# Blocks 3 to 5: half of the first product by 49 small products instead of 7 large ones

## The chip, the core and the metric

The kernel runs on one NeuronCore of a Trainium2 chip. TensorE (PE) multiplies matrices; VectorE (DVE), ScalarE (ACT) and GpSimd (POOL) do elementwise work; SyncE (SP) issues DMAs, and so do the queues of ACT and POOL. Matrix products land in PSUM, which has eight banks of 128 x 512 fp32; everything else lies in SBUF, or in DRAM (HBM). The metric is the device time of one execution in microseconds, as the median of the runs; lower is better.

## What is computed

```
state = gamma * state + k_t^T v_t          (4 batches, 8 heads, 768 steps, head size 64)
y_t   = (q_t state) / 8
x = y as (3072 tokens, 512)
h = x @ w_in                               (512 x 2048)
out = (h * sigmoid(1.702 h)) @ w_out       (2048 x 512)
```

All in fp32. The recurrence is computed in chunks of 128 steps (small attention-like products, 64x64); the two large products take most of the time.

## The kernel before, in words

Tokens are worked in six blocks `m` = 0 to 5 of 512 tokens (as four quarters). Chunk steps of the recurrence that make x for a later block are run between units of work of the current block (`between`, L968 to L980: `step` and `turn`).

**First product ("up").** w_in is laid out as eight column blocks `p`; two of them make a pair `d` (0 to 3). Of x and of w_in, four quadrants are held, plus sums of them, so that a 2x2 block product takes seven products instead of eight (P1 to P7, a Strassen-Winograd scheme; `sums_x` L529 makes the sums of x, `sums_w1` L521 those of w_in). In blocks 2 to 5, `up(d)` (L555 to L597) runs the seven products of a pair, each of four matmuls with 256 columns (L562), adds the results in PSUM and in SBUF (ACT copies P1, P6 and P7 out, L569, L576, L583; DVE adds, L572, L580, L586, L588), applies the gate x*sigmoid(1.702x) on ACT (`hidden`, L393), and lastly makes, on DVE, the sums of the gated values that the second product needs (L594, L595 inside 128-column parts, L596, L597 between the four quadrants `G[.., s, :]`). In this text those are "presums" and "outer sums".

The last two pairs' weights (`W1B`) share their room with `ring` and `own`, the buffers of the second product; so from block 3 on they are fetched again from DRAM (`W1D`, L984, L988) on POOL's queue, 1792 KB each.

**Second product ("down").** In blocks 2 to 5, `down49` (L643) goes one level deeper: each of the seven products is again split by seven, so 49 products of 128x128x128 parts. A unit is half of one of the seven: four products or three of them, each of four matmuls with 128 columns (`products`, L662 to L667). `derive(i)` (L651) makes three sums of G on DVE for product i; the three sums of w_out are streamed from DRAM (`stream`, L632, 768 KB). Results are copied by ACT (`then`, L698) or added by DVE and POOL and stored (`put`, L683). `sums_g_outer` (L621) are further DVE sums between units. After units 1, 4, 7 and 10 a chunk step stands in the order of PE.

**Order.** PE runs in the order in which the program is written. For the other engines a planner orders the instructions at compile time, by program order and by when it reckons each to be ready; `keep_in_program_order` (`pin`, L118, while `ordered[0]` holds) keeps an instruction in its written place among the others so marked on its engine. Each engine runs its list strictly in order.

PSUM: two banks of tag x and two of tag y (`ps`), two double banks `pa` and `py` for the chunk steps (`ps_a`).

## Time and profile before

| what | us |
|---|---|
| runs (median of 3) | 658.35 (658.05, 658.35, 664.67) |
| span of the profiled execution | 660.5 |
| PE busy | 642.2 (97%) |
| DVE / ACT / POOL busy | 453.9 / 159.0 / 198.8 |
| block 3, first product (362.90 to 411.20) | 48.3 |
| block 3, second product with chunk steps (411.20 to 464.70) | 53.5 |
| block 5, second product, no chunk steps (613.20 to 660.50) | 47.3 |

The page gives no time of the profiled execution but its span, which is 2.15 us over the median of the runs; differences between stages are read from the span's clock. A fp32 matmul shows as two records, so the counts of matmuls in a row are twice those in the code. The duration of one instruction is longer than the distance between two of them when they overlap in the pipeline.

### The profile page before, as it was taken

The page shows a single profiled execution, that of the slowest core. Times are in us where ns is not written, and L with a number is a line of the kernel's source. Part 1 is how long each engine was busy: PE and PEld are TensorE (multiplying, and loading weights), DVE is VectorE, ACT ScalarE, POOL GpSimd, SP SyncE. Part 2 cuts the span into 40 slices and gives each one's busy share as a digit, 9 for nine tenths or more (in the row PEclk, how much of TensorE's full clock was granted, in tenths as well). Part 3 has the DMA queues.
Part 4 walks back from the last instruction along what each step waited for, and adds up shares of the span by engine and source line. Part 5 has one row for each costly group of instructions (what it writes and reads, how often), then busy time and mean ns, then how long its engine had stood idle before and what let it go on. Part 6 is the DMA issues. An engine that isn't in the chain of part 4 may idle for free.

```text
span 660.5 us, 15291 instructions
## 1 busy us (share of the span) xinstructions
PE 642.2 (97%) x6390; PEld 580.2 (88%) x6390; DVE 453.9 (69%) x645; ACT 159.0 (24%) x306; POOL 198.8 (30%) x225
## 2 busy tenths in 40 slices
PE   6789999999999999999999999999999999999997
PEld 3778888888788888889999888999888999988997
DVE  3699989999936973556984445995354995254965
ACT  4674233551000000333100233010233110233110
POOL 6400311310379217000536400445600255500000
PEclk9989999999999999999999999999999999999999
DMA  9995549763233556262485832386742252602142
GB/s 176 193 274 173 152 104 241 172 163 60 49 82 135 137 149 153 58 248 96 118 199 134 279 57 97 86 223 135 225 118 97 66 154 104 235 21 96 55 154 96
DMA packets 148149, 91.86 MB, mean 139 GB/s; under 512 B 131600, under 2 KB 134416, under 8 KB 147056
## 3 DMA queue, kind: packets, MB, share of 16 engines
q1 hardware_dynamic: 135856, 45.19, 29.8%
q0 software_dynamic: 9888, 44.46, 20.6%
q10 hardware_dynamic: 2336, 1.25, 0.6%
q8 instruction: 50, 0.82, 0.5%
q14 instruction: 19, 0.16, 0.1%
HBM read 72.89 MB, written 15.47 MB: 134 GB/s over the span
## 4 chain that ended last, share of the span: by engine, by line
PE 89%; DVE 4%; DMA 4%; SPq 1%; issue 1%; ACT 0%; DVEq 0%
PE pq L666 27%; PE px L562 17%; PE pd L799 13%; PE py L562 13%; PE ph L491 7%; PE ph L414 5%; PE pa L289 2%; PE py L312 2%; PE pa L297 2%; PE py L306 2%; DMA W<-in_moe_w_in_dram 1%; DMA W<-in_moe_w_out_dram 1%; DMA q_in<-in_q_dram 1%; PE pt L250 1%; SPq L140 1%
## 5 line engine op out<-in xcount | busy, mean ns | idle before, releaser
L635 POOL DMA_DIRECT2D ring<-W2D x28 | 15.4, 551 | 227.7 <-PE px L562 118.3
L666 PE MATMUL pq<-W,G 128*128 128x128 f32 x672 | 80.2, 276 | 0.0
L666 PEld LDWEIGHTS pq<-W,G 128*128 128x128 f32 x672 | 77.6, 192 | 1.3 <-issue 0.7
L666 PE MATMUL pq<-ring,own 128*128 128x128 f32 x448 | 60.1, 276 | 1.3 <-issue 1.3
L562 PE MATMUL px<-X,W1A 128*128 128x256 f32 x256 | 59.8, 379 | 0.0
L562 PE MATMUL px<-X,W1B 128*128 128x256 f32 x256 | 59.8, 379 | 0.0
L666 PEld LDWEIGHTS pq<-ring,own 128*128 128x128 f32 x448 | 54.5, 192 | 0.4
L562 PEld LDWEIGHTS px<-X,W1B 128*128 128x128 f32 x256 | 48.5, 190 | 6.7
L562 PEld LDWEIGHTS px<-X,W1A 128*128 128x128 f32 x256 | 48.4, 190 | 6.5
L393 ACT ACTIVATE G<-G 128x512 f32<-128x512 f32 x60 | 37.4, 628 | 54.7 <-DVE G L572 33.4
L799 PE MATMUL pd<-W,G 128*128 128x256 f32 x224 | 49.6, 381 | 0.0
L799 PEld LDWEIGHTS pd<-W,G 128*128 128x128 f32 x224 | 42.2, 190 | 5.9
L562 PE MATMUL py<-X,W1A 128*128 128x256 f32 x192 | 45.4, 379 | 0.0
L562 PE MATMUL py<-X,W1B 128*128 128x256 f32 x192 | 45.4, 379 | 0.0
L562 PEld LDWEIGHTS py<-X,W1A 128*128 128x128 f32 x192 | 36.5, 190 | 5.0
L562 PEld LDWEIGHTS py<-X,W1B 128*128 128x128 f32 x192 | 36.5, 190 | 5.0
L580 DVE TENSOR_TENSOR t<-py,u 128x512 f32<-128x512 f32 x16 | 11.1, 692 | 32.3 <-PE py L562 32.3
L569 ACT ACTIVATE p<-px 128x512 f32<-128x512 f32 x16 | 9.6, 597 | 96.0 <-PE px L562 96.0
L414 PE MATMUL ph<-X,W1A 128*128 128x256 f32 x128 | 30.6, 397 | 0.9 <-DVE X L347 0.9
L594 DVE TENSOR_TENSOR G<-G 128x512 f32<-128x512 f32 (+2 forms) x24 | 12.3, 513 | 25.7 <-ACT G L393 25.7
L666 PE MATMUL pq<-ring,G 128*128 128x128 f32 x224 | 29.6, 275 | 0.0
L666 PE MATMUL pq<-W,own 128*128 128x128 f32 x224 | 29.6, 275 | 0.0
(237 smaller groups left out, 1226.0 us busy)
## 6 DMA issues: line engine op xcount, KB each, us to landing
ring<-W2D POOLq DMA_DIRECT2D x28, 768.0 KB, 4.8
W1B<-W1D POOLq DMA_DIRECT2D x6, 1792.0 KB, 9.8
W<-in_moe_w_in_dram SPq DMA_DIRECT2D x12, 512.0 KB, 5.9
W<-in_moe_w_out_dram SPq DMA_DIRECT2D x10, 512.0 KB, 5.8
out_dram<-o POOLq DMA_DIRECT2D x20, 256.0 KB, 3.0
q_sq<-in_q_dram SPq DMA_DIRECT2D x144, 32.0 KB, 2.1
k_sq<-in_k_dram SPq DMA_DIRECT2D x144, 32.0 KB, 2.1
v_in<-in_v_dram SPq DMA_DIRECT2D x72, 64.0 KB, 3.1
```

The lines of the kernel that those rows point to most:

```text
L289: pe.matmul(pa[HALF[w], u, 0, s, :], kt[HALF[u], w, s, :], qt[HALF[u], w, s, :], start=True, stop=True)
L297: pe.matmul(pa[HALF[u], w, 1, s, :], kd[HALF[w], HP * u + s, :], vn[HALF[w], HP * u + s, :], start=True, stop=True)
L306: pe.matmul(py[HALF[o], u, 1, 2 * w + s2, :], old[HALF[u], w, 2 * s2 + o, :], qt[HALF[u], w, 2 * s2 + o, :], start=True, stop=True)
L312: pe.matmul(py[HALF[o], w, 0, 2 * u + s2 if f < NEW else 2 * s2 + u, :], vn[HALF[w], HP * u + s, :], a[HALF[w], u, s, :], start=True, stop ...
L393: pin(act.activation(g, h[:, i], AF.Gelu_apprx_sigmoid))
L414: pe.matmul(h[:, ab], w, X[:, 2 * th + c // 2, c % 2, :], start=(ab == 0 and c == 0), stop=(c == 3), skip_group_check=True)
L491: pe.matmul(acc[:, u, :], w, x, start=(start and u == 0 and c == 0), stop=(stop and c == 1), skip_group_check=True)
L562: pe.matmul(acc[:, u, :], t[:, q1 + u, sa, c, :], X[:, sb, c, :], start=(start and u == 0 and c == 0), stop=(stop and c == 1), skip_group_ ...
L594: dve.tensor_sub(q[0][1], q[0][0], q[0][1])
L635: pool.dma_start(c, W2D[i])
L666: pe.matmul(p0[:, j, :], a[:, d], w[:, d], start=(new and j == 0 and d == 0), stop=(d == NP // 2 - 1), skip_group_check=True)
L799: pe.matmul(p0[:, n, :], g1(m, p, sa)[:, n * P:(n + 1) * P], W2[:, sb, p, :], start=(new and p == 0 and n == 0), stop=(last and p == NP - ...
```

## The change

In blocks 3 to 5, pairs 0 and 1 keep their seven plain products; pairs 2 and 3 go by 49 products of 128x128x128 parts each. `up_mixed` replaces the four calls of `up`; its order on all engines is written by hand (`ordered[0] = True`). Block 2 still runs `up` for all four pairs and makes the new sums of weights for pairs 2 and 3 (`inner_w1`), which go to DRAM (`T1D`, `Q1D`).

What is added, in the order of a block:

- weights: 14 fetches of three 128x128 parts per product and pair (`fetch_t`, 192 KB each), three of the plain pairs' sums (`fetch_q(s, True)`, 512 KB each) and three more of the inner ones into the same place, all on SP; before, it was two of 1792 KB on POOL.
- sums of x for the inner level, on DVE (`inner_x`, five operations each for X0/X1, X2/X3 and X4 to X6).
- 14 plain products: P1 of pair 0, P1 of pair 1, P2 of pair 0, and so on in the order P1, P2, P6, P5, P7, P4, P3. The P1 of pair 0 is copied into the bank of P2, which accumulates on it, so one DVE addition goes.
- 14 inner products of seven matmuls with 128 columns (`quarters`), pairs 2 and 3 in turn; P1 seeds the banks of P2 the same way. Results come as seven parts, four into G and three into a buffer E; `post` adds them (five operations on two quadrants at once or on one), then `gate`, `presum`, `outer`. `post` of pair 2 is on POOL, that of pair 3 on DVE.
- the first two `derive`s of the second product are pinned into this order; its first stream goes by SP.

`down49` loses one kept sum (`t`): product 5 now accumulates in the banks of product 4. `ring`, `own` and `W1B` become one tile `LATE`, whose parts are given out by hand.

```diff
-    W1A = const.tile([P, NP // 2, 7, 2, P], F32, name="W1A")
-    W1B = [late.tile([P, 2, 7, 2, P], F32, name=f"W1B{i}", tag=f"late{i}") for i in range(2)]
+    W1A = const.tile([P, NP, 4, 2, P], F32, name="W1A")
+    LATE = late.tile([P, 2 * NP * 3, P], F32, name="LATE")
...
+    def fetch_t(k):
+        d, sw = 2 + k % 2, OF[SEQ[k // 2]][0]
+        tag = ("kT", "at", "qT", "L", "kn", "kT", "at", "M", "qT", "L", "kn", "at", "M", "L")[k]
...
+        pin(sp.dma_start(t, T1D[d][:, {5: 4, 4: 5}.get(sw, sw)]))
...
+    def up_mixed(loads, turn_next, first_stream, second_stream, derive_first, derive_second):
...
+        def quarters(p0, prod, d, half):
...
+            pairs = [(a12, b21), (s2, t2), (s3, t3), (d0, t1)] if half == 0 else [(a11, b11), (d2, t4), (d1, b22)]
+            new = prod in ("P1", "P5")
+            for j in ((0, 2, 1, 3) if half == 0 else (0, 2, 1)):
+                x, w = pairs[j]
+                pe.matmul(p0[:, j, :], w, x, start=(new and j == 0), stop=True, skip_group_check=True)
...
+        def post(eng, d, s):
...
+            pin(eng.tensor_add(top, top, m1))
+            pin(eng.tensor_add(h1u0, h1u0, h0u1))
+            pin(eng.tensor_add(one_e(2), one_e(2), h1u1))
+            pin(eng.tensor_add(h1u1, h1u1, h1u0))
+            both = at(b + 1, d, [*K, [7 * P, 2]])
+            pin(eng.tensor_add(both, both, E[:, :, 1:3] if K else E[:, k, 1:3]))
...
+        for n in range(14):
+            prod, d = SEQ[n // 2], n % 2
...
+            if prod == "P1":
+                if d:
+                    save(("p", d), "s3", x)
+                else:
+                    pin(act.activation(y, x, AF.Copy))
...
+        for k in range(14):
+            prod, d = SEQ[k // 2], 2 + k % 2
...
+            for half in range(2):
+                quarters(p0[half], prod, d, half)
+                if d == 2:
+                    evacuate(half)
+            if d == 3:
+                evacuate(0)
+                evacuate(1)
+            if prod in ("P7", "P3"):
+                s, name = (3, "v") if prod == "P7" else (2, "u")
+                for half in range(2):
+                    pin(dve.tensor_add(place(d, s, half), out(y[half], half), out(kept[name, d][half], half)))
...
+            if k == 0:
+                inner_x(1)
+            elif k in (2, 3):
+                presum(k - 2, ALL)
+                outer(k - 2)
+            elif k == 8:
+                post(pool, 2, A)
+            elif k == 9:
+                first_stream()
+                post(dve, 3, A)
+                gate(3, A)
+                gate(2, A)
+            elif k == 10:
+                turn_next()
+                presum(3, A)
+                post(pool, 2, (1,))
+            elif k == 11:
+                post(dve, 3, (1,))
+                presum(2, A)
+                derive_first()
+                gate(3, (1,))
+                gate(2, (1,))
+                loads[1]()
+            elif k == 13:
+                second_stream()
+                post(pool, 2, (2,))
+                post(dve, 3, (2,))
+                presum(3, (1,))
+                presum(2, (1,))
+                gate(3, (2,))
+                gate(2, (2,))
+                derive_second()
+                presum(3, (2,))
+                outer(3)
+                presum(2, (2,))
+                outer(2)
...
-        if m > 1:
-            if m > 2:
-                W1B[:] = [late.tile([P, 2, 7, 2, P], F32, name=f"W1B{i}", tag=f"late{i}") for i in range(2)]
-                pool.dma_start(W1B[0], W1D[0])
+        if m == 2:
             for d in range(NP // 2):
+                if d > 1:
+                    inner_w1(d)
                 up(d)
...
+        elif m > 2:
+            prev = (m + 1) * CB
+            ordered[0] = True
+            up_mixed(
...
```

`k` counts the inner products: k = 8 and 9 are P7 of pairs 2 and 3, 10 and 11 are P4, 12 and 13 are P3. `A` stands for quadrants 0 and 3. `evacuate` copies P7 to a kept buffer and P4 (quadrant 1) to G and E, both on ACT.

## The prediction

> **What bounds the kernel now.** I read the page's shares first, then the chain in order of time, then the busy times by stage.
>
> ```profile
> PE 642.2 (97%) x6390; PEld 580.2 (88%) x6390; DVE 453.9 (69%) x645; ACT 159.0 (24%) x306; POOL 198.8 (30%) x225
> ```
>
> PE is busy nearly always. The chain in order of time says how fast it goes (start, length, work; two records make a matmul):
>
> ```profile
> 409.49 1.73 PE px L562 x8
> 411.22 6.25 PE pq L666 x56
> ...
> 613.16 43.78 PE pq L666 x392
> ```
>
> A plain product of four matmuls with 256 columns takes 1.727 us (the mean of the 28 between 362.87 and 411.22), 0.432 a matmul. In the second product 196 matmuls with 128 columns take 43.78 us, 0.2234 each. From the last plain product to the first unit of the second there is no gap: the chain goes on at 411.22. The stages of block 3 (busy time of PE, PEld, DVE, ACT, POOL; clock; DMA share; GB/s):
>
> ```profile
> 362.90:411.20 48.30, 48.30 (x226) 42.51 (x225) 21.90 (x34) 16.40 (x27) 9.42 (x13) 1.00 0.49 148
> 411.20:464.70 53.50, 52.85 (x906) 52.02 (x905) 42.65 (x64) 3.87 (x7) 25.84 (x29) 1.00 0.57 140
> ```
>
> So PE is saturated in both at a granted clock of 1.00, DVE is half idle in the first product and 80% busy in the second. Why there is no gap at the seam is seen in the timeline:
>
> ```profile
> 410.91 0.43 DVE L594 TENSOR_TENSOR G<-G 128x256 f32<-128x256 f32 x1 [0.69 <-ACT G L393]
> 411.06 2.84 PE L666 MATMUL pq<-W,G 128*128 128x128 f32 x24
> 411.25 0.60 ACT L393 ACTIVATE G<-px 128x512 f32<-128x512 f32 x1 [0.37 <-PE px L562]
> 411.26 0.69 DVE L655 TENSOR_TENSOR own<-G 128x512 f32<-128x512 f32 x1
> 411.86 0.42 DVE L595 TENSOR_TENSOR G<-G 128x256 f32<-128x256 f32 x1
> 412.20 0.29 DVE L594 TENSOR_TENSOR G<-G 128x128 f32<-128x128 f32 x1
> ```
>
> Quadrant 0, which the first unit reads, was gated and presummed while the last three products still ran; one `derive` is already running. DVE then works without a pause until 436. Any DVE work that arrives late here is felt by PE.
>
> **What the change saves.** Per pair, 28 x 0.4317 = 12.09 us become 49 x 0.2234 = 10.95: 1.14 saved, 2.28 per block with two pairs, 6.85 in three blocks. That is all that PE can save, 1.04%: 651.5. The removed additions (P1 of three pairs, `t`) and POOL's two issues (0.58 each) lie beside PE and are worth nothing.
>
> **What it costs at the seam.** Let 0 be the moment when PE ends the last inner product. P7 of pair 3 (k=9) ends four products, 28 matmuls, earlier: -6.25. What follows is one chain, since the written order on ACT is copies of P7, gate of pair 3, gate of pair 2, and only then the copies of P4. A product is seen by ACT 0.19 after PE moves on (411.06 against 411.25 above). Then: second copy 0.49 (128x384, as L704), addition 0.55 (128x384, L709), `post` of pair 3 on two quadrants 2 x 0.69 + 3 x 0.42 = 2.64 (512 and 256 columns), two gates of 1024 columns at 1.17 (L207's 128x1024), first copy of P4 0.60. Sum 6.81, so it ends at +0.56. The first unit of the second product wants tag x's banks, which that copy frees: **0.56 late**. Then three copies (0.49 + 0.60 + 0.49), `post` of pair 3, quadrant 1 (2 x 0.42 + 3 x 0.29 = 1.71), and the first presum of pair 2 (0.42), which stands behind it on DVE: +4.27. PE needs it after ten matmuls, at 0.56 + 2.23 = 2.79: **1.48 more**.
>
> Unit 2 needs quadrant 1. DVE's queue before it: presum 0.42, first `derive` 3 x 0.60 (distance of such rows), four additions of P3 2.12, `post` of quadrant 2 1.71, three presums 0.87: 6.92, so +11.19. PE needs it at 2.04 + 3.57 + 2.68 (units 0, 1) + 2.0 (chunk step, 417.40 to 419.42) + 2.23 = 12.5. Bare, 1.3 us to spare; but the planner mixes the chunk step's four DVE operations (2.4) and half an outer sum (1.14, L626's distance) in between, as it mixes L655 between L594 and L595 above: **2.2 late**. Unit 4 needs the outer sums of both pairs: 0.29 + 1.80 + 0.58 + 1.41 + 0.58 + 1.41 = 6.1 bare, up to 9.3 with `put`'s additions 1.06 and two halves of outer sums 2.28; PE comes after 1.34 + 2.68 + 0.45 = 4.5. Between 1.6 and 4.8, I take **3.2**. After unit 4 DVE's list is that of before, with the derives of two products done. Sum of waits without any mutual slowing: 7.4 per block.
>
> **The shared work of POOL.** `post` of pair 2 puts two operations of 1.27 (L531, 128x512) and three of 0.74, then twice 2 x 0.74 + 3 x 0.45 = 2.8, on POOL: 10.4 us, beside DVE's densest stretch. What such neighbours do to each other:
>
> ```profile
> 368.90 0.74 POOL L694 TENSOR_TENSOR o<-o 128x256 f32<-128x256 f32 x1
> ...
> 426.37 1.64 POOL L692 TENSOR_TENSOR o<-o 128x256 f32<-128x256 f32 x1 [3.61 <-DVE o L687]
> 427.34 1.21 DVE L655 TENSOR_TENSOR own<-G 128x512 f32<-128x512 f32 x1
> 428.94 0.68 DVE L656 TENSOR_TENSOR own<-G 128x512 f32<-128x512 f32 x1
> ```
>
> Alone, the POOL operation takes 0.74 and the DVE one 0.68; beside each other 1.64 and 1.21. But over block 3's second product the loss is small: L655 to L657 lie 0.16, 0.05 and 0.05 above their 0.69 in the mean, 1.8 us for seven of each, beside some 16 us of POOL work. By that ratio 10.4 us of POOL cost DVE 1.2; if each blocked the other throughout, the gate of pair 2 would come 2.0 later (POOL's 4.8 from -6.6 and DVE's 2.64 in turn end at +0.8, and gate and copy at +2.6 instead of 0.56), and DVE would lose POOL's later 5.6 and the chunk step's 2.1 as well: nearly 10. Nearest to it is the measured ratio; with half of the 2.0, because the first two `post`s coincide from end to end, I take 2.1.
>
> SBUF — State Buffer, section "Who interferes with whom", of the Trainium skill speaks against the change: a DVE operation with two SBUF inputs and a GpSimd operation that reads SBUF exclude each other for a whole instruction. The row at 426.37 looks like that (it began to move when L628 ended at 427.34). By that rule alone the upper sum just given would hold; by the ratio the lower.
>
> **The other parts.** The plain pairs' sums (three of 512 KB) can't be fetched before the last unit of the previous block has read their place; P6 of pair 0 wants the first at 4 x 1.727 = 6.9 us. 256 KB landed in 3.0 (out), 768 KB in 4.8 (ring): about 4 plus 0.6 of issue, 2.3 to spare; rows of 512 KB at the start took 4.6 to 9.1, so the bounds are 0 and 2.8 a block. I take 0. The inner fetches have 4.7 us between the release of their place and use, three products, against 3; SP's 16 small loads (8 in 4.0 us, so 8) stand behind the first fetches and before the inner ones, which have 20 us. Block 2's added DVE work (eight operations, about 5.5) and POOL work (eight) lie in a first product where DVE is busy 25.5 of 48.4: nothing; without that cover at most the 0.6 of the last one.
>
> **Sum.** Per block 7.4 + 2.1 - 2.28 = 7.2 us; three blocks 21.7. From the span 660.5 to 682; from the median, 2.15 lower, **680**.
>
> **Rivals.** (1) *All waits are hidden*, the saving comes whole: 651.5. It is one mechanism: the planner and the pipelines shorten the chain on ACT and DVE behind P7. It decides when that chain takes 6.25 us or less to the copy of P4 and the DVE list behind it no more than PE's 2.2 us to the presum; I come to 6.81 and 3.71. For it: ACT operations follow each other at 0.48, below their 0.60. Against: the chain is of dependent steps, which don't overlap. (2) *Only the first unit waits*: 2.04 against 2.28, so 657.6, if the planner keeps the chunk steps' DVE work out; with small port losses to 664. (3) *Full mutual blocking*: with 2.0 + 2.7 + 2.7 + 2.1 for the port and unit 4 at its upper 4.8, the waits come to 18.5, net 16 a block: 707. Gaps over 3 us could also lower the granted clock, which the page shows at 9 and 8 tenths only in the first slices; the price would be the same order. (4) *Late fetches*: 2.8 a block on top, 8 us, with any of these. That the products don't become 49 would show in the count of matmul records, and I see no room for it in the code.
>
> **How the numbers follow.** The forecast (some waits at three units, 665 to 703) gets 0.66; rival 2 (652 to 664) 0.18; rival 1 0.07; rival 3 beyond 703 0.09. The range reaches from 655 to 703: it takes in the forecast and the upper part of rival 2, and leaves out the outer two. About 1% is what a measurement of this kernel tells from no change: faster than 651.8 gets 0.05 (651.5 is barely there), slower than 664.9 gets 0.75, between 0.20.
>
> **What would show it.** In the changed profile: inner products at 1.56 us each (7 x 0.2234); the first product of a block 46.1 long instead of 48.3; PE idle before the first unit of the second product, released by ACT's copy of P4, then by DVE's presum; again at units 2 and 4, released by DVE; `post` on POOL above 1.27 and 0.74. If PE shows no idle time after the seam, the chain is shorter than I sum it; if it is idle inside the plain products, the fetches are late; if POOL's `post` runs at its lone times, the share for blocking is wrong.

## The result, and the profile after

| | median us | runs | profiled span |
|---|---|---|---|
| before | 659.8 | 658.1 to 664.7 | 660.5 |
| after | 709.5 | 707.7 to 712.4 | 706.8 |

The changed kernel is slower by a ratio of 1.0755 (95% interval 1.0704 to 1.0806). The forecast was 680, its range 655 to 703. The direction was right and the time 29 us too low. Ratios here and below are to executions of the kernel before that were run beside the kernel in question (medians 659.5 to 662.5 us), without executions more than 1.5% slower than the fastest of their kernel; the medians in us are of all executions.

The page's busy times of the changed kernel, first row, with the granted clock of TensorE in 40 slices of the span:

```profile
PE 652.4 (92%) x6642; PEld 597.0 (84%) x6642; DVE 492.4 (70%) x738; ACT 174.9 (25%) x342; POOL 238.3 (34%) x269
...
PEclk9899999999999999999999999999999899998899
```

PE was busy 97% before and is 92% now, though there is less for it to do; and its clock falls to 8 tenths in slices late in the run, where it had stood at 9 or more. Where that is, the stages of block 3 say (busy time of PE, PEld, DVE, ACT, POOL, with instructions; clock; DMA share; GB/s):

```profile
368.50:414.80 46.30, 46.29 (x310) 43.05 (x308) 22.48 (x37) 16.21 (x30) 14.99 (x16) 1.00 0.57 170
414.80:418.40 3.60, 0.17 (x2) 0.00 (x0) 3.02 (x6) 2.48 (x4) 0.08 (x1) 0.96 0.11 16
418.40:434.40 16.00, 12.67 (x204) 12.11 (x204) 14.51 (x27) 4.64 (x10) 10.17 (x14) 0.90 0.58 145
434.40:445.80 11.40, 6.38 (x40) 6.19 (x40) 10.71 (x20) 0.00 (x0) 5.44 (x6) 0.83 0.56 131
445.80:450.60 4.80, 4.78 (x32) 4.67 (x32) 4.80 (x7) 0.00 (x0) 0.00 (x0) 0.69 0.45 89
450.60:484.80 34.20, 34.20 (x633) 33.76 (x633) 22.80 (x34) 2.18 (x4) 17.41 (x21) 1.00 0.67 166
```

The first product has no gap and takes 46.3 us instead of 48.3: the saving is there. The loss lies in the 36 us after it. PE's rows that begin with a wait (start, length, work; in brackets the idle time and what ended it):

```profile
418.46 3.94 PE L958 MATMUL pq<-W,G 128*128 128x128 f32 x20 [3.49 <-ACT G L840]
422.85 0.71 PE L958 MATMUL pq<-W,G 128*128 128x128 f32 x4 [0.46 <-DVE G L760]
434.47 0.71 PE L958 MATMUL pq<-W,G 128*128 128x128 f32 x4 [2.88 <-DVE G L760]
445.82 3.92 PE L958 MATMUL pq<-W,G 128*128 128x128 f32 x20 [4.96 <-DVE G L766]
...
429.09 2.50 PE L958 MATMUL pq<-W,G 128*128 128x128 f32 x20
```

The four places and their releasers are those of the prediction: ACT's copy of P4 ahead of unit 0, presums ahead of unit 0's end and of unit 2, the outer sum ahead of unit 4. They sum to 11.8 us. Note also the lengths: twenty records took 3.94 and 3.92 us behind a wait, where the twenty at 429.09, behind none, took 2.50. That is a second price of these waits.

Blocks by the first plain product on PE, in us, each from the one profiled execution of its kernel; the experiments stand below it for reference:

| kernel | block 2 begins | block 2 | block 3 | block 4 | block 5 | median, all |
|---|---|---|---|---|---|---|
| before | 261.4 | 101.3 | 101.9 | 100.1 | 95.9 | 659.8 |
| after | 268.0 | 100.5 | 116.3 | 115.1 | 106.9 | 709.5 |
| e1 stores behind | 259.5 | 100.7 | 116.5 | 115.3 | 107.0 | 701.7 |
| e2 no POOL `post` | 265.3 | 101.2 | 112.7 | 111.8 | 103.5 | 697.4 |
| e3 no `post` | 267.6 | 102.2 | 99.8 | 102.0 | 93.5 | 666.9 |
| e4 early quadrant | 259.8 | 101.0 | 116.6 | 112.2 | 103.3 | 695.3 |
| e5 all `post` on DVE | 267.4 | 100.6 | 123.0 | 116.3 | 106.2 | 710.5 |
| e6 early and late | 258.9 | 102.0 | 115.7 | 107.8 | 97.0 | 681.6 |
| e7 late others | 259.6 | 101.0 | 119.4 | 115.2 | 102.7 | 698.5 |
| e8 fill, eleven | 265.5 | 100.9 | 118.2 | 117.9 | 107.0 | 711.3 |
| e9 fill, five | 268.3 | 101.4 | 114.7 | 113.2 | 106.1 | 705.1 |
| e10 joint, a | 257.8 | 101.0 | 107.9 | 106.0 | 94.6 | 671.4 |
| e11 joint, b | 260.4 | 100.7 | 102.5 | 101.4 | 94.6 | 662.6 |
| e12 joint, c | 263.1 | 100.5 | 103.7 | 102.4 | 95.2 | 671.1 |

After against before: 46.3 us of span, of which 5.8 arise ahead of block 3 and 14.4, 15.1 and 11.0 in blocks 3 to 5. Block 5 has no chunk steps, so its length is the cleanest measure of the seam between the two products. Kernels that are alike up to block 2 begin it up to 5 us apart (257.8 to 263.1 in the rows of e1, e4, e6, e7 and e10 to e12), for a reason that was not looked for.

### The profile page after: what moved, and what is told of

Its sections match the earlier page's. It is cut to its first block, busy times and chain, and to the rows that moved or that the text cites. A ratio compares the mean times of both kernels' runs of the same rounds, so it can differ in the third digit from the quotient of the medians.

```text
span 706.8 us, 16061 instructions
## 1 busy us (share of the span) xinstructions
PE 652.4 (92%) x6642; PEld 597.0 (84%) x6642; DVE 492.4 (70%) x738; ACT 174.9 (25%) x342; POOL 238.3 (34%) x269
## 4 chain that ended last, share of the span: by engine, by line
PE 64%; DVE 15%; DMA 9%; SPq 3%; issue 3%; POOL 3%; ACT 2%; DVEq 0%; POOLq 0%
PE pq L958 22%; PE pw L678 10%; PE pd L1089 7%; PE ph L495 7%; PE pw L706 7%; PE px L610 4%; PE py L610 3%; DMA v_in<-in_v_dram 2%; DMA W<-in_moe_w_in_dram 2%; DMA W2D<-X 2%; DMA W<-in_moe_w_out_dram 1%; SPq L166 1%; DVE G L746 1%; DMA q_in<-in_q_dram 1%; PE ph L420 1%
## 5 line engine op out<-in xcount | busy, mean ns | idle before, releaser
L958 PE MATMUL pq<-W,G 128*128 128x128 f32 x672 | 92.0, 296 | 31.3 <-DVE G L766 13.0
L958 PE MATMUL pq<-LATE 128*128 128x128 f32 x448 | 62.0, 283 | 0.0
L958 PEld LDWEIGHTS pq<-LATE 128*128 128x128 f32 x448 | 56.7, 198 | 0.4
L420 PEld LDWEIGHTS ph<-X,W1A 128*128 128x128 f32 x256 | 48.0, 190 | 7.8 <-DVE X L355 1.2
L678 PE MATMUL pw<-X,W1A 128*128 128x256 f32 x192 | 42.4, 379 | 0.0
L678 PEld LDWEIGHTS pw<-X,W1A 128*128 128x128 f32 x192 | 36.3, 190 | 4.8
L746 POOL TENSOR_TENSOR G<-G,e 128x512 f32<-128x512 f32 x3 | 3.8, 1262 | 97.6 <-DVE e L852 97.6
L1089 PE MATMUL pd<-W,LATE 128*128 128x256 f32 x160 | 35.1, 380 | 0.0
L1089 PEld LDWEIGHTS pd<-W,LATE 128*128 128x128 f32 x160 | 30.3, 190 | 4.1
L958 PE MATMUL pq<-LATE,G 128*128 128x128 f32 x224 | 31.9, 289 | 0.0
L678 PE MATMUL pw<-X,LATE 128*128 128x256 f32 x144 | 31.6, 380 | 0.0
L958 PE MATMUL pq<-W,LATE 128*128 128x128 f32 x224 | 29.8, 276 | 0.0
```

What stands on the lines that cost most here:

```text
L420: pe.matmul(h[:, ab], w, X[:, 2 * th + c // 2, c % 2, :], start=(ab == 0 and c == 0), stop=(c == 3), skip_group_check=True)
L678: pe.matmul(p0[:, u, :], w1(2 * d + u, sw)[:, c, :], X[:, sx, c, :], start=(start and u == 0 and c == 0), stop=(stop and c == 1), skip_gro ...
L746: pin(eng.tensor_add(top, top, m1))
L958: pe.matmul(p0[:, j, :], a[:, d], w[:, d], start=(new and j == 0 and d == 0), stop=(d == NP // 2 - 1), skip_group_check=True)
L1089: pe.matmul(p0[:, n, :], g1(m, p, sa)[:, n * P:(n + 1) * P], W2[:, sb, p, :], start=(new and p == 0 and n == 0), stop=(last and p == NP - ...
```

## The experiments

### Block 1: a store that waits at the head of a queue

Block 1 was not touched by the forecast, yet block 2 begins 6.6 us later. VectorE's in-order queue shows where (`inner_w2`, which needs X's room back from a store of `W2D`); after:

```profile
223.52 0.69 DVE L907 TENSOR_TENSOR X<-W 128x512 f32<-128x512 f32 x1 [13.06 <-DMA W2D<-X]
```

Before, the same instruction waited 3.32 us:

```profile
215.51 0.69 DVE L612 TENSOR_TENSOR X<-W 128x512 f32<-128x512 f32 x1 [3.32 <-DMA W2D<-X]
```

SP's queue (start, time it took, what) says why the store was late, after and then e1:

```profile
211.61 0.57 SPq L568 DMA_DIRECT2D Q1D<-LATE  x1
212.23 0.62 SPq L569 DMA_DIRECT2D Q1D<-LATE  x1
215.53 0.51 SPq L568 DMA_DIRECT2D Q1D<-LATE  x1
216.13 0.58 SPq L569 DMA_DIRECT2D Q1D<-LATE  x1
216.81 9.20 SPq L908 DMA_DIRECT2D W2D<-X  x2
```

```profile
201.19 16.71 SPq L908 DMA_DIRECT2D W2D<-X  x3
```

The planner had taken four stores of block 2's `inner_w1` forward to block 1, ahead of the store. They wait for POOL's `sums_w1`, and everything behind them on SP waits with them. e1 holds those four, and nothing else:

```diff
-        sp.dma_start(Q1D[:, :, 2 * d - 4], W1L[:, 0, :, 2 * d - 4])
-        sp.dma_start(Q1D[:, :, 2 * d - 3, 1], b22)
+        tc.keep_in_program_order(sp.dma_start(Q1D[:, :, 2 * d - 4], W1L[:, 0, :, 2 * d - 4]))
+        tc.keep_in_program_order(sp.dma_start(Q1D[:, :, 2 * d - 3, 1], b22))
```

> Nothing is left out; only SP's order changes: the four stores of `Q1D` that wait for POOL's sums of `w_in` (two of 384x1x256, two of 384x1x128) are held behind block 1's `W2D` stores, at their place in the text in block 2. PE's, DVE's, ACT's and POOL's orders are those of the changed kernel. Theory (in block 1 those stores stood at the head of SP's queue ahead of a `W2D` store, so X's room came free late and DVE's L907 waited 13.06 us instead of 3.32): DVE's wait at L907 falls back to about 3 to 4 us, the stretch before block 2 loses 6 to 8 us, blocks 3 to 5 keep their lengths; 701 to 704 us. Rival (block 1 is longer because of the added DVE and POOL work for the products' operands): no change, 708 to 711.

Measured: 701.66 us, inside the range expected; ratio to before 1.0619 (1.0584 to 1.0653). The wait at L907 is 3.29 us again, block 2 begins 8.5 us earlier, and blocks 3 to 5 keep their lengths within 0.2. The theory holds: about 7 to 8 us were SP's order. Over all rows of the table, the six kernels with the changed kernel's order on SP begin block 2 at 267.0 in the mean (265.3 to 268.3), the seven with e1's edit at 259.9.

### What the additions cost: e2, e3 and e5

e2 leaves out POOL's `post` of pair 2 (the three calls of `post(pool, 2, ..)`). e3 leaves out the three of DVE too. e5 leaves out nothing and gives pair 2's to DVE:

```diff
-                post(pool, 2, A)
+                post(dve, 2, A)
...
-                post(pool, 2, (1,))
+                post(dve, 2, (1,))
...
-                post(pool, 2, (2,))
+                post(dve, 2, (2,))
```

> Left out: POOL's fifteen additions per block after the inner products of pair 2 (its inner parts are not added up); the orders of PE, DVE and ACT are those of the changed kernel. Theory (POOL's additions and DVE's shut each other out, one instruction at a time): DVE's five additions for pair 3's quadrants 0 and 3 fall from 5.3 us to the 2.6 that I worked out, PE's wait ahead of unit 0 falls from 3.49 us to 0.8 to 1.3, the waits at units 2 and 4 from 7.8 to 4 to 6, and the slow clock that follows the gaps becomes less: 6 to 9 us per block, 682 to 692 us in all. Rival 1 (DVE's additions are slow by their own strides, with or without POOL): they stay at 5 us and the time above 703. Rival 2 (it is POOL's own lateness that the gates of pair 2 wait for, not DVE): DVE's additions stay as they are, yet unit 0 comes earlier.

> Left out: all additions after the inner products, those of pair 2 on POOL and those of pair 3 on DVE. Theory (the 2.2 us that the products save per block are whole, and what the block loses is the chain additions, gates, sums and the clock after each gap): unit 0 waits under 0.5 us, units 2 and 4 together 1 to 4, the clock stays at 0.95 or more through the seam, blocks 3 to 5 each take 98 to 104 us; with block 1's 8 us still there, 660 to 673 us. Rival (fetches and the smaller products themselves cost what was lost): blocks 3 to 5 stay above 108 us, over 690 in all.

> Nothing is left out; the additions of pair 2 go from POOL to DVE, which then has both pairs' additions one after the other. Theory (DVE and POOL take turns anyway, so POOL's hand is worth next to nothing): two times five additions for quadrants 0 and 3 take 2 x 2.64 = 5.3 us on DVE alone, what the one pair's takes now beside POOL; unit 0 waits 3 to 4.5 us, and the time stays within 1% of the changed kernel's, 703 to 716 us. Rival (the slowing by POOL is small and something else sits in those 5.3 us): DVE gets 6 us more work per block on the chain and the time rises by 9 to 18 us, 718 to 728.

Measured: e2 697.44 (1.0558, 1.0518 to 1.0599), e3 666.91 (1.0077, 1.0049 to 1.0106), e5 710.50 (1.0759, 1.0717 to 1.0800).

First the additions themselves. In the timeline of the changed kernel, DVE's five for pair 3's quadrants 0 and 3, and POOL's rows beside them:

```profile
410.57 1.12 DVE L746 TENSOR_TENSOR G<-G,e 128x512 f32<-128x512 f32 x1
411.73 0.83 DVE L747 TENSOR_TENSOR G<-G 128x256 f32<-128x256 f32 x1
412.49 1.49 DVE L748 TENSOR_TENSOR e<-e,G 128x256 f32<-128x256 f32 x1
414.01 1.15 DVE L749 TENSOR_TENSOR G<-G 128x256 f32<-128x256 f32 x1
415.19 0.69 DVE L751 TENSOR_TENSOR G<-G,e 128x512 f32<-128x512 f32 x1
...
410.42 0.73 POOL L748 TENSOR_TENSOR e<-e,G 128x256 f32<-128x256 f32 x1
411.23 1.05 POOL L749 TENSOR_TENSOR G<-G 128x256 f32<-128x256 f32 x1
412.36 1.33 POOL L751 TENSOR_TENSOR G<-G,e 128x512 f32<-128x512 f32 x1
413.65 1.22 POOL L367 TENSOR_TENSOR state<-state,whole_h 128x512 f32<-128x512 f32 x1
```

From 410.57 to 415.88 is 5.31 us. The same five in e2, with POOL's `post` gone and only its state update (L367, 408.48 to 409.95) left beside them:

```profile
408.36 0.69 DVE L746 TENSOR_TENSOR G<-G,e 128x512 f32<-128x512 f32 x1
409.09 1.15 DVE L747 TENSOR_TENSOR G<-G 128x256 f32<-128x256 f32 x1
410.16 0.41 DVE L748 TENSOR_TENSOR e<-e,G 128x256 f32<-128x256 f32 x1
410.60 0.42 DVE L749 TENSOR_TENSOR G<-G 128x256 f32<-128x256 f32 x1
411.06 0.69 DVE L751 TENSOR_TENSOR G<-G,e 128x512 f32<-128x512 f32 x1
```

3.39 us, and each row that has nothing of POOL's beside it is at the 0.69 and 0.42 of the prediction; the one beside L367 is 0.73 over. So the slowing is POOL's, and both rivals of e2 fall, since each had DVE's additions stay as they were. PE's waits in block 3 become 1.57, 0.86, 1.80, 0.39 and 5.39: unit 0's is less than half, unit 4's is not smaller at all. Over a block the idle time falls by only 1.8, 1.7 and 1.8 us. That is why e2 came out at 697 and not at 682 to 692.

e5 shows the other side: DVE does the ten additions alone, in 2.67 and 3.39 us, and the kernel is as fast as with POOL's help (the intervals overlap). Two engines that take turns were worth one here. Block 3 of the profiled execution of e5, which was the longest of its four (715.3 us, the others 709.6 to 710.6), also has a wait of 3.06 us in its first product, of which more below.

The page "SBUF — State Buffer" of the Trainium skill, section "Who interferes with whom", says that a DVE operation with two SBUF inputs contends with a GpSimd operation that reads SBUF, and calls the ports that they share an exclusive lock. The 5.31 us against 2.67 alone (e5) agree with it, and so do the two PSUM-reading additions just ahead (L852 at 409.38 and 409.99, one input from PSUM, 0.69 and 0.55 us beside POOL's L746 and L747, which run from 408.39 to 410.46): with at most one input in SBUF, the section says, a DVE instruction like these does not contend with GpSimd.

e3 settles the other half. With no additions PE has no wait at the seam (1 to 4 us had been expected at units 2 and 4); in its stages of block 3 the clock stays at 1.00:

```profile
369.90:416.00 46.10, 46.10 (x311) 43.21 (x310) 22.16 (x42) 20.99 (x38) 7.02 (x9) 1.00 0.56 160
416.00:434.30 18.30, 18.30 (x273) 17.99 (x271) 18.05 (x32) 2.24 (x4) 5.82 (x7) 1.00 0.58 140
```

Blocks 3 and 5 are 2.1 and 2.4 us shorter than before the change, which is near the saving of 2.28 that was worked out. Block 4 is not, for another reason, seen in its first product:

```profile
478.83 12.29 PE L678 MATMUL pw<-X,LATE 128*128 128x256 f32 x48 [2.09 <-DMA LATE<-W1D]
```

The plain pairs' sums came late, and the records behind the wait are slow (48 records take 10.35 us at 0.2156 each). So the late fetch cost 2.1 + 1.9 here. In the changed kernel itself it never showed; it did in one block each of e3, e5, e6, e7 and e10, with 2.1 to 3.5 us of wait.

### The clock: e8 and e9

In block 3 of the changed kernel, 14.4 us lost + 2.3 saved - 11.8 idle leaves 4.9 us, in blocks 4 and 5 likewise 5.8 and 5.3: 16 us that no idle time explains. The granted clock in the trace does. It is either 1.00 or 0.50, and in each of the three blocks it stands at 0.50 for three stretches of 3.41 us; before the change it never does in these blocks. Two of block 3's (columns as above, each stretch at 0.50 behind the one ahead of it; the third is 418.09 to 421.50):

```profile
431.74:435.15 3.41, 0.68 (x6) 0.68 (x7) 3.41 (x9) 1.15 (x2) 2.14 (x2) 1.00 0.73 249
435.15:438.57 3.42, 3.42 (x19) 3.42 (x18) 3.42 (x9) 0.00 (x0) 0.00 (x0) 0.50 0.41 92
...
441.98:445.39 3.41, 0.00 (x0) 0.00 (x0) 3.34 (x5) 0.00 (x0) 2.87 (x3) 1.00 0.87 251
445.39:448.81 3.42, 2.99 (x14) 3.00 (x15) 3.42 (x6) 0.00 (x0) 0.00 (x0) 0.50 0.79 151
```

Nine stretches are 30.7 us at half the clock, 15.4 us of PE's work at most: nearly all of the 16. e3, whose matmuls are the same, kept PE busy for 99.2 us in block 3 and 90.0 in block 5, where the changed kernel took 104.5 and 95.4.

What lowers the clock is the next question. e8 and e9 fill PE's wait ahead of unit 4 with products that nobody reads, in blocks 3 and 4:

```diff
+                    if m in (3, 4) and half == 0 and i == 2:
+                        t = ps_a.tile([P, 8, P], F32, name="fill", tag="pa")[:, 0:4]
+                        for r in range(5):          # e8: 11
+                            tc.keep_in_program_order(pe.matmul(t.rearrange("p (a b) t -> p a (b t)", b=2), W2[:, 3, 0, 0:P],
+                                                               W2[:, 3, 0:2, :], start=True, stop=True, skip_group_check=True))
                     products(acc[x, half], pairs[i][half], i not in (2, 3, 5))
```

> Nothing is left out; the changed kernel with SP's stores where they were, and eleven products of 128x512 (about 0.43 us each, 4.7 together) whose results nobody reads, put on PE in blocks 3 and 4 alone where it waits 4.96 us ahead of unit 4; the orders of all other instructions are those of the changed kernel, and block 5 is the control. Theory (PE's clock falls after PE has stood idle, so the 4.8 us per block that the idle time does not explain are a second price of the gaps): with the gap filled the clock behind unit 4's start is 0.95 or more instead of 0.69, its first twenty products take 2.4 us instead of 3.9, and blocks 3 and 4 become 1.5 to 3 us shorter each, block 5 stays at 106.9; 703 to 707 us. Rival (the clock is low there for another reason, such as the load on the chip): no block changes by more than 0.5 us.

> Nothing is left out. As e8, with five filling products instead of eleven: in e8 each took 0.86 us, twice what I had reckoned, so that eleven outlasted the gap by 4.5 us; five take 4.3 us, a little less than the 4.96 us for which PE waits ahead of unit 4. In blocks 3 and 4 alone; block 5 is the control. Theory (PE's clock falls behind idle time): the first twenty products of unit 4 take 2.4 to 2.8 us instead of 3.9 and unit 4 itself starts when it did, 77.3 us into the block; blocks 3 and 4 are 1.0 to 2.0 us shorter each (116.3 and 115.1 before), block 5 stays at 106.9; 704 to 708 us, which the time alone hardly tells from no change. Rival (the clock is low there for another reason): unit 4's first products stay at 3.9 us and the blocks within 0.5 us.

Measured: e8 711.33 (1.0801, 1.0735 to 1.0867): a miss by my own reckoning, since a product of 128x512 takes 0.86 us and not 0.43, so the filling outlasted the gap and unit 4 began 3 us late; even so its first 24 records took 2.84 us. e9 705.05 (1.0663, 1.0630 to 1.0696). Its rows at the place:

```profile
441.09 4.46 PE L1043 MATMUL fill<-W 128*128 128x512 f32 x10
445.39 0.61 PE L958 MATMUL pq<-W,G 128*128 128x128 f32 x4
446.81 2.50 PE L958 MATMUL pq<-W,G 128*128 128x128 f32 x20 [0.82 <-DVE G L766]
```

Unit 4 goes on 77.1 us into the block, as before (77.3), but its twenty records take 2.50 us instead of 3.92. In block 4 the same twenty take 2.50 instead of 3.91. So the low clock there is the consequence of PE having stood idle. The lengths of the blocks say less: blocks 3 and 4 are 1.6 and 1.9 us shorter, but the control, block 5, moved by 0.8 itself, and by the granted clock block 3 still has three stretches at 0.50 (the one at unit 4 is gone, unit 0's wait is followed by two), block 4 one and block 5 two.

### Where the waits come from: e4, e7, e6

My prediction had one chain for each wait. The alternative is that there is only one: DVE's queue from the first addition after P7 to the outer sum, and PE pays for its length at whichever unit it meets first. e4 takes quadrant 0 (whose products end early) out of that queue, with all additions on DVE and the rest of the written order changed to suit; e7 takes out the work of others that the planner mixes in; e6 does both:

```diff
+            elif k == 5:                                  # e4, e6; all on DVE
+                post(dve, 2, (0,)); post(dve, 3, (0,))
+                gate(2, (0,)); gate(3, (0,))
+            elif k == 7:
+                presum(2, (0,)); presum(3, (0,))
+            elif k == 8:
+                post(dve, 2, (3,))
...
-                        if i in (0, 1, 3):                # e6, e7
-                            sums_g_outer((0, 1, None, 2)[i])
+                        if m > 2 and i in (2, 3, 4):
+                            sums_g_outer(i - 2)
...
-            if between and (n in (2, 5, 11, 16, 21) if m == 1 else n % 3 == (1 if m else 2)):
+            if 2 < m < NB - 1 and n == 3:
+                turn((m + 1) * CB + 1)
+            if between and (n in (2, 5, 11, 16, 21) if m == 1 else n in (4, 6, 8, 10) if m > 2 else n % 3 == (1 if m else 2)):
```

In e6 and e7 the evacuations and `derive`s of the first units, and `sums_g_outer`, are also pinned in written order. All three have e1's edit.

> Nothing is left out. SP's four stores are held as in e1, and quadrant 0 of the inner pairs, whose products end four pairs of products earlier, gets its additions, gate and sums by itself right then (all on DVE, which is idle there), quadrant 3 is done by itself when its own products end, and ScalarE copies the last product's results before the gates of quadrant 3. Theory (the outer sum that unit 4 waits for comes at the end of one DVE queue; in the changed kernel it ends 31 us after the last inner product, 16 later than PE could be at unit 4, and the waits at units 0 and 2 are only where that lateness is first paid): taking 3.4 us of additions and 0.8 of sums out of the queue, and the turns with POOL, makes unit 4 some 4 to 6 us less late per block; the waits at units 0 and 2 nearly vanish but that at unit 4 grows to 7 to 11 us; 684 to 692 us. Rival (each wait has its own chain): the waits at units 0 and 2 go, that at unit 4 stays at 5; 3 x (3.5 + 2.9 + 3 of slow clock) less than e1, 670 to 678 us.

> Nothing is left out. SP's four stores as in e1; the additions after the inner products stay as they are; in blocks 3 and 4 (and for the second product's sums in 5 too) the DVE work that nothing near needs is put behind the outer sum: the chunk step's four instructions (2.7 us) and its turn (1.4) by moving the chunk steps two to three units later, the second product's sums over outer pairs (2.4), and the evacuations of units 2 and 3 (1.2). Theory (the length of DVE's queue up to the outer sum sets unit 4's start): 7.7 us less in the queue, unit 4 is 6 to 8 us less late per block in blocks 3 and 4 and some 3 to 4 in block 5; 680 to 687 us, with the wait at unit 0 as it was (3 to 3.5 us). Rival (unit 4's lateness comes from the chain of additions, gates and sums itself, the mixed-in work only fills DVE's pauses): under 2 us per block, 695 to 702 us.

> Nothing is left out; e4's and e7's edits together. Theory (one DVE queue): what is left between the first sum after P7 and the last outer sum is 25.4 us by the sum of its instructions, begun 7.8 us ahead of the last inner product's end, so it ends 17.6 to 19 us behind it where PE could be at unit 4 after 12.7: one wait of 5 to 6 us per block is left, with some 2 us of slow clock behind it, against a saving of 2.2 on the products; 666 to 675 us. Rival (each wait has its own chain): no wait is left, 650 to 658 us, faster than before.

Measured: e4 695.31 (1.0532, 1.0472 to 1.0592), e7 698.52 (1.0602, 1.0542 to 1.0662), e6 681.55 (1.0333, 1.0286 to 1.0381). By time, all three missed their windows, and e7 fell into its rival's (695 to 702). By block 5, which has no chunk steps, e4 gained 3.7 us over e1 and e7 4.3 (3 to 4 by its theory, under 2 by its rival), and both together 10.0.

e4 in block 3 is a lesson: 116.6 us, nothing gained. PE's waits moved (1.33, 3.87, 4.53, 1.72 instead of 3.49, 0.46, 2.88, 4.96) and nearly kept their sum, and the stretches at half the clock became five. The outer sum there still ended 30.4 us after the last inner product, against 31.0: DVE's queue held entries that wait for PE, such as the evacuation of unit 3, ahead of the outer sum, and a late PE makes those late in turn. e7 in blocks 3 and 4 gained at unit 4 (1.55 us instead of 4.96 in block 3) and lost it elsewhere, as its moved chunk steps then waited for their loads:

```profile
466.05 1.13 PE L300 MATMUL pa<-qT,kT 64*64 64x64 f32 x32 [5.59 <-DVE kT L264]
```

e6 has DVE's queue clean. The stages from its first addition after P7 (399.3) over the last inner product's end (406.9) to the outer sum's end (424.1):

```profile
399.30:406.90 7.60, 7.60 (x70) 7.60 (x69) 7.32 (x17) 4.60 (x9) 1.20 (x1) 1.00 0.59 174
406.90:424.10 17.20, 13.86 (x120) 13.31 (x118) 16.45 (x46) 3.50 (x6) 1.67 (x3) 1.00 0.36 117
```

DVE has no pause of even 0.1 us in these 24.8 us (25.4 were reckoned), and ends 17.2 us behind the last inner product (17.6 to 19). Here the sum of one queue sets the start of unit 4, which follows the outer sum's end at once. PE's waits at the seam are 1.19, 0.79 and 1.49 in the place of one of 5 to 6 that was expected, and block 5 takes 97.0. What kept the time at 681 are block 3's chunk steps, moved too close to each other for their loads (waits of 1.71, 1.85, 4.73 and 0.93), and a fetch 3.27 us late in block 4.

### Shortening the queue: e10, e11, e12

e10 and e11 add up, gate and sum quadrants 1 and 2 of both inner pairs in single instructions, and fetch the plain pairs' sums first:

```diff
+            elif k == 11:
+                post2(1)                  # G[:, 4:8, 1] at once: 2.64 us instead of 2 x 1.71
+                gate(3, (3,))
+                gate2(1)
+                presum2(3)
...
+            elif k == 13:
+                second_stream()
+                presum2(1)
+                post2(2)
+                gate2(2)
+                derive_second()
+                presum2(2)
+                outer2()
...
-        for k in range(4):
-            fetch_t(k)
         for s in (5, 4, 6):
             fetch_q(s, True)
-        fetch_t(4)
+        for k in range(5):
+            fetch_t(k)
```

The turn and the chunk steps stand after units 2 and 4, 7, 9, 11 in e10; in e11 the turn is back in its old place and the steps come after units 3, 5, 8, 10.

> Nothing is left out. e6 with three edits: quadrants 1 and 2 of both inner pairs are added up, gated and summed in instructions that span both pairs (2.64 us instead of 2 x 1.71 for the additions, 0.84 instead of 1.2 for sums, 2.44 instead of 2.76 for the outer sum); the plain pairs' own `w_in` sums are fetched ahead of the inner pairs' first; the first chunk step of blocks 3 and 4 comes after unit 4, the others after units 7, 9 and 11, the turn after unit 2. Theory (one DVE queue sets unit 4's start): 2.8 us less in the queue, so some 1 to 2 us of waits per block in the place of 3.5; block 5, which has no chunk steps, 94 to 95.7 us (97.0 in e6, 95.7 before the change); blocks 3 and 4 100 to 105 if the chunk steps' loads come in time, the plain pairs' fetch no longer late; 656 to 666 us. Rival (the wait at unit 4 is a chain of latencies through PE, ScalarE and DVE that joining pairs makes longer): block 5 stays at 97 or above, over 670 in all.

> Nothing is left out. As e10, but the turn stays ahead of the outer sum, where the changed kernel has it (1.4 us of DVE in the queue, for earlier loads of the next chunks' q and k), and the chunk steps come after units 3, 5, 8 and 10. Theory: block 5 as in e10; in blocks 3 and 4 unit 4 comes 1.4 us later than in e10, against which the waits for the chunk steps' loads that e6 had (4.7 and 1.9 us in block 3) fall under 2; 655 to 666 us. Rival (those waits were DVE's backlog and not the loads): e11 is 2 to 4 us slower than e10.

Measured: e10 671.36 (1.0158, 1.0123 to 1.0193), e11 662.58 (1.0024, 1.0004 to 1.0044). Block 5 takes 94.6 in both, as forecast, and is the first block that is shorter than before the change with all its work in it. By time e10 missed its window (and is over 670, as its rival was to be, but without the rival's block 5 of 97); it lost its time by its chunk steps (1.02, 0.91, 1.57 and 1.52 of wait in block 3) and a fetch that was 2.39 us late in block 4 for all its place at the head of the queue. e11's earlier loads remove all but one of those; its rival, that the waits were DVE's backlog, falls, since it had e11 slower than e10. e11 is inside its window, and its blocks 3 to 5 have no stretch at half the clock. PE's waits of half a microsecond or more in e11's block 3 are two:

```profile
418.99 1.13 PE L986 MATMUL pq<-LATE 128*128 128x128 f32 x8 [1.76 <-DVE LATE L965]
431.36 0.69 PE L300 MATMUL pa<-qT,kT 64*64 64x64 f32 x32 [0.98 <-DVE kT L264]
```

e12 goes after the first of them by doing unit 3's operands ahead of quadrant 2's additions (and moves the second chunk step to unit 6):

```diff
                 presum2(1)
+                derive_second()
                 post2(2)
                 gate2(2)
-                derive_second()
+                presum2(3)
                 presum2(2)
```

> Nothing is left out. As e11, with two edits: the operands of unit 3 are worked out ahead of quadrant 2's additions instead of behind them, quadrant 3's sums fill DVE's wait for quadrant 2's gate in their stead, and the second chunk step of a block comes after unit 6 instead of 5. Theory (PE has a date for each entry of DVE's queue, and the order by date decides what is left): the waits of e11 at unit 3 (1.76 and 1.53 us) and at the second chunk step (0.98 and 0.97) go, at unit 4 under 1 us takes their place; blocks 3 and 4 come from 102.5 and 101.4 us to 99 to 101, block 5 stays at 94.6; 654 to 661 us, level with the kernel before or up to 1% under it. Rival (what is won at unit 3 is lost at unit 4, as when the waits at units 0 and 2 were taken away): 661 to 664 us.

Contrary to that text, e12 does change the computation: unit 3's operands are written into the room where quadrant 2's inner parts still lie, so those parts are lost; the instructions and their number are those of e11. Measured: 671.12 (1.0114, 1.0072 to 1.0156). The waits at unit 3 and at the chunk step are gone, and a larger one stands ahead of unit 4, with slow records behind it (20 in 3.45):

```profile
427.43 3.45 PE L986 MATMUL pq<-W,G 128*128 128x128 f32 x20 [2.04 <-DVE G L795]
```

The time is over both windows. The rival holds in kind: putting the entries of one queue in another order moved the wait and didn't remove it. The executions lie between 664 and 675 us; why they spread so is open.

No version beat the kernel before. e11 is level with it, at 0.2% above, with 2.3 us per block saved on PE and as much lost in what is left of the waits.

## Why the prediction was wrong

The forecast put 21.7 us on three blocks; the spans differ by 46.3. The 24.6 between them, by the prediction's own terms:

| term | forecast | measured | difference |
|---|---|---|---|
| saving on PE, three blocks | -6.85 | 2.1 and 2.4 a block in e3; first product 46.1 | about 0 |
| idle time of PE at the seam | 3 x (7.4 + 2.1) = 28.5 | 11.8 + 11.5 + 8.0 = 31.3 | +2.8 |
| clock after the waits | named in rival 3, priced 0 in the sum | 4.9 + 5.8 + 5.3 left over; by the granted clock up to 15.4 | +16.0 |
| blocks 1 and 2 | "nothing" | block 3 begins 5.8 later | +5.8 |

**What the change saves**: right, to 0.1 us, per product (1.56 us), per first product (46.1) and, where no wait hid it, per block (e3).

**Unit 0, "0.56 late"**: right releaser, wrong size, 3.49. From P7's end on PE to the copy that frees the bank I had 6.81 us; it took 9.9 (408.53 to 418.41). Three terms: pair 3's P7 is copied only when both its halves are done (ACT begins at 408.75), and two additions follow the first copy, so copies and additions took 2.0 instead of 1.2; DVE's `post` took 5.31 instead of 2.64; the gates took 2.0 instead of 2.3, since they overlap. Half of the port's upper bound for this chain, 1.0, had been taken; 2.67 was measured, of which POOL's state update, left out of my list of neighbours here, has about 0.7 by e2.

**Units 0's end, 2 and 4, "1.48, 2.2 and 3.2"**: measured 0.46, 2.88 and 4.96 in block 3, with 1.5 and more taken already by unit 0's lateness. The sum is near, but the picture of separate chains was not what the runs support: e4 and e12 show waits that move when one of them is taken away, and e6 that the sum of DVE's queue gives the end of the outer sum to about half a microsecond. (Two of the sums are 0.1 off: the upper end at unit 4 comes to 9.4 and not 9.3, the port's term to 2.2 and not 2.1.)

**The port, 2.1 per block**: near as idle time, for another reason than mine. Without POOL's `post` PE idles 1.8, 1.7 and 1.8 us less in blocks 3 to 5 (e2 against after): in block 3 unit 0 waits 1.9 us less, the others together as long as before. For unit 0's chain the bound by full blocking, 2.0, was the better guide than the ratio, which came from a stage where DVE and POOL had slack. The blocks are 10.4 us shorter, 3.5 a block, since the stretches at half the clock also fall from three to two in each block. Full blocking throughout, 9.5 a block, is not what was measured.

**The sum** is the step that failed most. It adds idle time and has no term for what PE does just after. Rival 3 said that gaps over 3 us could lower the clock at "the same order" of price, and then the sum took none of it; by e9 twenty records behind one gap took 1.4 us longer than with the gap filled, and three such stretches a block make about 5. That missing term is 16.0 of the 24.6 us.

**Block 2's added work, "nothing"**: right for block 2 (100.5 against 101.3) and for the engines that I looked at. SP was not costed at all: not what its new stores wait for, nor that the planner may take them forward past another's. e1 shows 7 to 8 us there.

**Fetches, 0**: right in the changed kernel; but the 2.3 us to spare were not a margin. In five of the twelve experiments one block's fetch was 2.1 to 3.5 us late, about my upper bound of 2.8, with up to 1.9 of slow clock on top. What made those fetches late was not looked for.

**Rivals**: rival 3's total, 707, is nearest to 709.5, and for another reason than its own: its waits were to come to 18.5 us a block, and 8.0 to 11.8 were measured; 5.3 of clock and 5.8 us ahead of block 3 made up the rest. Rivals 1 and 2, with 0.25 between them, did not happen.

## What to carry to other kernels

Where one engine has no pause between a producer's end and its reader, sum its whole queue from the last pause to the entry that is waited for and compare that with the reader's time: a wait that is taken away elsewhere on that queue only moves. Give every wait of TensorE of some two microseconds or more a second price (here up to 1.7 us for each 3.41 us at half the clock), and look, for each DMA that is added, at what it waits for and what stands behind it on its queue. Elementwise work put on a second engine that takes turns with the first was no help here, where both began together.

## What the runs showed of the hardware

The slow records behind a wait don't follow from its length alone. After 1.49 us of idle time (and two shorter waits just before) 18 records took 2.27 us in blocks 3 and 5 of e6 and 3.66 in block 4; after 2.04 and 1.99 (e12) twenty took 3.45 and 4.13, where 2.50 is usual; after 2.09 (e3) 48 took 12.29, but after 3.27 (e6, block 4) only 10.60.

They follow from where a wait falls. From 100 us on, in all fourteen profiles, the granted clock changes only at points of a grid of 3.41 us that stays fixed through the profile (in block 3 of the changed kernel it falls at 418.09, then 5 and 8 steps later). Cut by that grid, there are 2328 stretches at a clock of 1.00. All 49 with 2.0 us or more of idle PE were followed by one at 0.50, and none of the 2258 with less than 1.75; of the 21 between, seven were. e6 shows the same waits on both sides of the line (behind each stretch's length stands PE's busy time):

```profile
420.04:423.46 3.42, 1.90 (x15) 1.52 (x13) 3.23 (x8) 0.00 (x0) 0.53 (x1) 1.00 0.27 54
423.46:426.87 3.41, 2.65 (x23) 2.65 (x24) 3.40 (x5) 0.00 (x0) 1.88 (x2) 1.00 0.45 181
...
539.50:542.92 3.42, 1.63 (x13) 1.24 (x11) 3.21 (x8) 0.00 (x0) 0.53 (x1) 1.00 0.32 72
542.92:546.34 3.42, 2.94 (x14) 2.94 (x15) 3.42 (x5) 0.00 (x0) 1.88 (x2) 0.50 0.38 158
```

The wait of 3.27 us in e6, which was free, was cut by a point of the grid, at 484.89, and left 1.28 and 1.98 us of idle time on its two sides. The page "TensorE: Matmul & The Clock Gate" of the Trainium skill, section "HAM oscillation — how this bites in real kernels", puts the rule at idle gaps of about 3.4 us, and the section "What's actually happening" calls the window that watches PE free-running. The fixed grid agrees with such a window; that some 2 us inside one stretch are enough does not agree with the threshold, and the runs decide.

A fp32 product with 512 columns takes 0.86 us from start to start, with 256 columns 0.432 and with 128 0.2234: 1.75 ns a column in the short row and 1.68 in the long one.
